# Attention with a SOLU block on one core: an allowance in TensorE's order, VectorE at some casts and low parts, and new wanted times

## The chip, the core and the metric

The kernel runs on one core of a Trainium2 chip. The metric is device time in microseconds from launch to end, the median of several runs. TensorE multiplies matrices into PSUM (eight banks of 128 x 512 fp32). VectorE, ScalarE and GpSimd work on PSUM and SBUF, GpSimd on SBUF alone in this kernel, and SyncE issues the DMAs. Each engine takes its own instructions in the order in which the program has them and waits at semaphores for the others.

## What is computed

```python
factor = 2; scale = 1.0 / np.sqrt(D)                       # B, H, S, D = 4, 8, 1152, 64
q_pool = q.reshape(B, H, S // factor, factor, D).mean(axis=3)
scores = scale * np.matmul(q_pool, k.transpose(0, 1, 3, 2))
attn = np.exp(scores - np.max(scores, axis=-1, keepdims=True))
attn = attn / (np.sum(attn, axis=-1, keepdims=True) + 1e-09)
x = np.matmul(attn, v).transpose(0, 2, 1, 3).reshape(B * S // 2, H * D)   # 2304 x 512

h = x @ w_in                                               # 512 -> 1024
e = np.exp(h - np.max(h, axis=-1, keepdims=True))
solu = h * e / (np.sum(e, axis=-1, keepdims=True) + 1e-09)
mu, var = mean and variance of solu over its 1024 columns
out = ((solu - mu) / np.sqrt(var + 1e-06) * g_ln) @ w_out  # 1024 -> 512
```

q and k are drawn with a large spread, and all inputs and the output are fp32.

## The kernel before

**The work.** There are 32 heads, taken as 16 pairs P. A head has 576 pooled queries and 1152 keys, and its keys are cut into nine blocks of 128. A *step* is one block of keys of one head, so there are 288 steps, s = 9 g + j for block j of head g. To keep fp32's accuracy at TensorE's speed, numbers are split in a high part and a low part (the rest), and products are made of high by high, high by low and low by high.

**One step** (`scores`, from line 958) is this: TensorE makes the scores of 128 keys by 576 queries as two halves of 288 columns, each of two products (`product`; the second product adds the low parts and the shift by the row's maximum). ScalarE takes exponentials: one writes `eh`, the fp16 high part, another writes `e32` (printed as `e`), the same in fp32. GpSimd subtracts (`rest`, line 1006): `e32 - eh`, the *low part*, stored beside `eh`. In some steps `eh` is not a second exponential but a cast of `e32` by VectorE (`cast`, line 996; `use_dve` says in which steps). Then TensorE multiplies `eh`, its low part and the two parts of v (`vhi`, `vlo`) for two or three steps at a time (`values`). In the first steps both halves of a step's scores lie in a pair of banks and one exponential takes all 576 columns (`expo2`, line 989, steps below TP); later one takes 288 columns (`expo`, line 983). `eh` has six buffers, `e32` two. From head 8 on (AH) a low part is written as 512 and 64 columns.

**Before a head's steps** come its maxima (`maxima`): 12 or 15 products of 384 columns into three banks, each reduced by VectorE (line 860), then the transpose of the row maxima (line 869), the shift `c` by VectorE (line 872) and two small DMAs. **Before a pair's steps** come its loads and splits (`pair`): k is transposed and split, q is loaded, pooled by GpSimd (line 606, "q's sum"), transposed and split, and v is scaled by its own largest value and split. For v, the letter VM of the pair says which engines do it: B scales on ScalarE (line 794), C on VectorE (line 796), both with the high part on ScalarE (line 803) and the low part on GpSimd (line 812); with A, ScalarE scales and makes the high part in one (line 801) and VectorE the low part (line 808).

**The token block** (`tokens`) takes 128 rows of x at a time, 18 blocks. A block is 24 products of 512 columns with the parts of w_in, exponentials, statistics, a scaling by g (line 1212), transposes, and 24 products with the parts of w_out. Thirteen blocks are done beside the steps, five after them (the tail). **The weights** (`weight_part`) come in 16 parts; each takes two ScalarE instructions `up` and `un` (line 486), a join on GpSimd (line 493), two VectorE instructions (lines 497, 501), a copy on ScalarE (line 504, `wih` or `woh`) and a subtraction on VectorE.

**What sets the order.** Nothing is written in the order in which it runs. Each piece of work is given to `add` with its engine, an estimated length and a wanted time `at`, counted in steps; `Plan.run` then plays the program forward with these lengths and with `HOP`, an allowance in ns for a signal from one engine to another. Whenever an engine is free, it takes the piece with the smallest `at` whose inputs are there by that play and whose buffers are free; pieces more than `win` steps ahead of the current scores must wait. The instructions are written out in the order that results. So the numbers in `KP` and the lengths change the order of the instructions of every engine, and on the chip only this order is left of them. The wanted times in `KP` are: W (first part of the weights, spacing of the first eight, of the others), M and MA (first block, spacing, length of a block's first products), P (how many steps ahead of a pair's first step k, q and v are prepared and loaded: KA, QA, VA, LK, LQ, LV), N, N1 (maxima: how far ahead, over how many steps), AV (delay of `values`), OF (offsets within a head's end and a block), V0 (v of pair 0), and TP and TX (steps below which scores use paired or extra banks).

## Time and profile before

| | |
|---|---|
| median of 3 runs | 707.68 us (705.69 to 709.21) |
| profiled execution | 707.37 us, its span from first to last instruction 705.1 us |
| busy share of the span | TensorE 95%, weight loads 83%, ScalarE 78%, VectorE 72%, GpSimd 72% |
| chain that ended last | TensorE 66%, VectorE 12%, ScalarE 10%, GpSimd 6%, issue 5% |
| DMA | 75.8 MB, mean 107 GB/s |

The span is the time that the trace covers; the 2.3 us between it and the execution's time lie around it. TensorE's busy time is the union of its matmuls' spans, and these overlap: the next matmul starts while the last is still running out. So a gap in its work is seen as idle time only when it is longer than that overlap. Weight loads are listed apart; a weight load that waits shows that TensorE had to wait for an input, at times without an idle gap among the matmuls. For the other engines too a span is longer than the distance to the next start when the engine is full, and the distance is then what an instruction costs.

### The profile page before, as it was taken

To read this page: it belongs to the slowest core of one execution; us is meant where nothing else is said; L and a number is where in the kernel's file an instruction comes from. 1 tells how busy PE (TensorE), PEld (TensorE's weight loads), DVE (VectorE), ACT (ScalarE), POOL (GpSimd) and SP (SyncE) were. 2 spreads that over 40 slices of the span, in tenths; PEclk is the share of its full clock that TensorE was granted. 3 is DMA by queue.
4 is the path that set the end of the run, shared out by engine and by line. 5 is a ranking of instruction groups with operands and counts; after the bars stand their busy time and mean duration, and the time that the engine had idled before them with its cause. 6 is when DMAs were issued, how large, how long until landed. Compare 5 with 4: busy or idle time off the path is not lost.

```text
span 705.1 us, 19052 instructions
## 1 busy us (share of the span) xinstructions
PE 672.5 (95%) x7151; PEld 582.0 (83%) x7151; DVE 509.0 (72%) x1216; ACT 551.3 (78%) x1366; POOL 507.8 (72%) x651
## 2 busy tenths in 40 slices
PE   9889889989999999999999999999999999999996
PEld 8677778778978888888888988898888898888775
DVE  7798888888878586777868686868686867235452
ACT  3989899988898797878888788888787877763432
POOL 2688899997788787787869686977868677751211
PEclk9999999999999999999999999999999999999999
DMA  5598576965271634546252635444344410010011
GB/s 181 162 211 200 154 190 164 252 143 140 68 163 44 148 90 104 134 93 152 52 138 61 145 85 125 113 91 116 72 121 101 104 34 19 16 24 16 15 31 30
DMA packets 76024, 75.80 MB, mean 107 GB/s; under 512 B 58789, under 2 KB 58909, under 8 KB 75933
## 3 DMA queue, kind: packets, MB, share of 16 engines
q1 hardware_dynamic: 75932, 74.60, 43.7%
q8 instruction: 56, 0.92, 0.6%
q14 instruction: 36, 0.29, 0.1%
HBM read 37.22 MB, written 4.72 MB: 59 GB/s over the span
## 4 chain that ended last, share of the span: by engine, by line
PE 66%; DVE 12%; ACT 10%; POOL 6%; issue 5%; ACTq 0%; DVEq 0%; POOLq 0%
PE bank L419 59%; POOL eh L1006 5%; DVE mx L860 4%; PE bank L1225 2%; ACT e L983 2%; DVE q L422 2%; PE bank L1375 2%; PE bank L628 1%; ACT eh L983 1%; ACT e L989 1%; ACT eh L989 1%; ACT q L722 1%; ACT e L1168 1%; PE bank L712 1%; DVE bank L497 1%
## 5 line engine op out<-in xcount | busy, mean ns | idle before, releaser
L1006 POOL TENSOR_TENSOR eh<-e,eh 128x64 f16<-128x64 f32 (+1 forms) x504 | 405.0, 828 | 109.7 <-ACT e L983 28.8
L860 DVE TENSOR_REDUCE mx<-bank 128x1 f32<-128x384 f32 x420 | 220.5, 548 | 50.5 <-PE bank L419 47.8
L419 PE MATMUL bank<-q,w 128*128 128x288 f32 (+1 forms) x1152 | 238.3, 312 | 6.7 <-ACT e L989 3.3
L419 PEld LDWEIGHTS bank<-q,w 128*128 128x128 f32 (+1 forms) x1152 | 184.6, 191 | 34.8 <-ACT e L983 12.1
L983 ACT ACTIVATE eh<-bank 128x288 f16<-128x288 f32 x392 | 167.0, 429 | 49.1 <-PE bank L419 46.1
L983 ACT ACTIVATE e<-bank 128x288 f32<-128x288 f32 x434 | 183.4, 433 | 16.7 <-POOL eh L1006 13.1
L419 PEld LDWEIGHTS <-eh 128*128 128x128 f16 x4104 | 134.0, 98 | 18.4 <-issue 8.3
L419 PE MATMUL bank<-vhi,eh 128*128 128x65 f16 x2664 | 144.2, 195 | 3.0 <-POOL eh L1006 2.9
L419 PE MATMUL bank<-w,q 128*128 128x384 f32 x390 | 132.9, 367 | 9.8 <-DVE mx L860 5.7
L419 PE MATMUL bank<-vlo,eh 128*128 128x64 f16 x1440 | 140.4, 193 | 0.0
L419 PEld LDWEIGHTS bank<-w,q 128*128 128x128 f32 x390 | 71.7, 190 | 25.6 <-DVE mx L860 13.4
L1208 POOL TENSOR_TENSOR st<-st 128x1 f32<-128x1 f32 x54 | 25.4, 471 | 58.4 <-ACT junk L1195 56.2
L989 ACT ACTIVATE eh<-bank 128x576 f16<-128x576 f32 x70 | 47.5, 680 | 3.5 <-PE bank L419 3.4
L989 ACT ACTIVATE e<-bank 128x576 f32<-128x576 f32 x71 | 48.4, 681 | 0.7 <-POOL eh L1006 0.4
L1156 DVE TENSOR_REDUCE st<-bank 128x1 f32<-128x512 f32 x36 | 24.7, 687 | 25.4 <-PE bank L419 22.5
L422 DVE TENSOR_TENSOR klo<-bank,khi 128x384 fp32r<-128x384 f32 x45 | 24.8, 552 | 19.1 <-ACT khi L631 18.9
L422 DVE TENSOR_TENSOR q<-bank,q 64x384 fp32r<-64x384 f32 (+2 forms) x63 | 28.8, 458 | 12.6 <-ACT q L722 9.7
L419 PE MATMUL bank<-woh,lh 128*128 128x512 f32 x104 | 33.3, 408 | 0.7 <-DVE e L1175 0.7
L419 PE MATMUL bank<-wih,xh 128*128 128x512 f32 x104 | 33.3, 407 | 0.0
L419 PE MATMUL bank<-wil,xh 128*128 128x512 f32 x104 | 32.9, 398 | 0.0
L419 PE MATMUL bank<-wih,xl 128*128 128x512 f32 x104 | 32.3, 397 | 0.0
L419 PE MATMUL bank<-woh,ll 128*128 128x512 f32 x104 | 32.1, 397 | 0.0
(128 smaller groups left out, 1025.1 us busy)
## 6 DMA issues: line engine op xcount, KB each, us to landing
qt<-in_q_dram SPq DMA_DIRECT2D x16, 576.0 KB
kt<-in_k_dram SPq DMA_DIRECT2D x32, 288.0 KB
vt<-in_v_dram SPq DMA_DIRECT2D x16, 576.0 KB
w<-w SPq DMA_DIRECT2D x32, 288.0 KB
w<-khi SPq DMA_DIRECT2D x30, 288.0 KB
w<-klo SPq DMA_DIRECT2D x30, 288.0 KB
out_dram<-o SPq DMA_DIRECT2D x36, 128.0 KB
raw<-in_moe_w_in_dram SPq DMA_DIRECT2D x8, 511.6 KB
```

Of the source, the lines that this page charges most:

```text
L419: nc.tensor.matmul(out=o, lhsT=a, rhs=b, start=first, stop=last, skip_group_check=True)
L422: nc.vector.tensor_tensor(out=o, in0=a, in1=b, op=ALU.subtract)
L497: nc.vector.tensor_scalar(out=ps.bitcast(I32), in0=tl["raw", n][:, :, 0], scalar1=5, scalar2=128 << 23, op0=ALU.logical_shift_right, op1=A ...
L628: nc.tensor.transpose(ps[:, c, :], tl["kt", P][:, 3 * i + c].rearrange("p h d -> p (h d)"), ident)
L860: nc.vector.tensor_reduce(out=tl["mx", g][:, m, c:c + 1], in_=tl["nps", (g, m, c)], op=ALU.max, axis=AXX)
L983: nc.scalar.activation(out=tl[name, (g, j)][:, f * HALF:(f + 1) * HALF], in_=tl[tn(j, f), (g, j, f)], func=ACTF.Exp, scale=ESC,)
L989: nc.scalar.activation(out=new((name, (g, j)), [128, SQ * 4 // mybir.dt.size(dtype)], dtype)[:, 0:SQ].rearrange("p (f i) -> p f i", f=2), ...
L1006: nc.gpsimd.tensor_tensor(out=e[:, o:o + c.stop - c.start], in0=e32[:, c], in1=e[:, c], op=ALU.subtract)
L1156: nc.vector.tensor_reduce(out=st(f), in_=tl[H_[f]], op=ALU.max, axis=AXX)
L1208: nc.gpsimd.tensor_tensor(out=st(o), in0=st(a), in1=nhalf if b is None else st(b), op=op)
L1225: nc.tensor.transpose(ps[:, c, :], tl[E][:, o:o + 128], ident)
L1375: plan.warm = lambda i: nc.tensor.transpose(bank[:, i, 0:128], ident, ident)
```

## The change

The numbers of `KP` are set anew, four names are new in it, and three pieces of code use them:

- **HP** = [145872, 60]: on work that TensorE takes up after 145.872 us of the play, 60 ns are added to the allowance for a signal from another engine to TensorE. It has no instruction of its own.
- **CD** is now a list of ranges. Casts by VectorE: steps 25 and 50 in 6 to 72, and every twentieth step from 80 to 280 (13). Before it was every tenth from 70 to 280 (22).
- **SD** names steps whose low part VectorE makes: 25, 38, 50 and 63. Its estimated length is VectorE's for 576 columns and 250 ns more.
- **MA** is the spacing of the first blocks; it has the same value as M's.
- VM: v is scaled on VectorE for the pairs 0, 1, 2, 3, 8, 12, 13 (before 1, 2, 3, 12), on ScalarE as B for 6, 7, 9, 10, 11, 14 (before 0, 6, 7, 8, 10, 11, 13), as A for 4, 5, 15 (before 4, 5, 9, 14, 15).

```diff
-KP = {'W': [2, 4.47, 5], 'step': 0.66, 'M': [78.27, 15.99, 7.61], 'TX': 112, 'TP': 71, 'win': 4.11, 'P': [22.92, 18.81, 13.57, 24.85, 27.38, 30.44], 'N': [10.43, 7], 'AV': 3.97, 'CD': [67, 10], 'VM': 'BCCCAABBBABBCBAA', 'AH': 8, 'OF': [5.14, 2.61, 11.19, 1.04, 2.66], 'N1': 12.32, 'warm': 1, 'ws': 1.3, 'GR': 1, 'GG': 10, 'b_eh': 6, 'b_w1': 4, 'V0': -55.58, 'VF': 1, 'QD': [0, 1], 'L0': 0.97, 'F': 0, 'DL': 2000}
+KP = {'W': [2, 5.8, 5], 'step': 0.73, 'M': [78.27, 15.99, 7.64], 'TX': 106, 'TP': 72, 'win': 4.6, 'P': [22.99, 20.5, 12.83, 24.85, 25.26, 30.44], 'N': [10.46, 6.38], 'AV': 4.07, 'CD': [[6, 73, 4], [73, 288, 5]], 'SD': [[15, 73, 8], [73, 288, 0]], 'VM': 'CCCCAABBCBBBCCBA', 'AH': 8, 'OF': [5.31, 2.61, 11.94, 0.25, 1.01], 'N1': 11.36, 'warm': 1, 'ws': 1.3, 'GR': 1, 'GG': 10, 'b_eh': 6, 'b_w1': 4, 'V0': -50.92, 'VF': 1, 'QD': [0, 1], 'L0': 0.97, 'F': 0, 'HP': [145872, 60], 'DL': 2000, 'MA': 15.99}
...
+        PAD = KP.get("HP", [0, 0])
+        pad = PAD[1]
...
-                            t = max(t, x.end + hop[x.engine][e] + load)
+                            t = max(t, x.end + hop[x.engine][e] + load + (pad if e == "PE" and t > PAD[0] else 0))
...
                     if o.engine == e and not m.deps[o]:
                         hop = 0
+                    elif e == "PE" != o.engine and t > PAD[0]:
+                        hop += pad
...
-    def use_dve(s):
-        a, b = KP.get("CD", [100, 0])
-        return s >= a and b > 0 and (s * b) % 100 < b
+    def use_dve(s, key):
+        return any(a <= s < z and (s * b) % 100 < b for a, z, b in KP[key])
...
-                add("POOL", POOL(SQ) + 149 * joined, a, lambda j=j: rest(j), [("eh", (g, j)), ("e32", (g, j))], [("eh", (g, j), "l")])
+                low = ([("eh", (g, j)), ("e32", (g, j))], [("eh", (g, j), "l")])
+                if use_dve(NJ * g + j, "SD"):
+                    add("DVE", DVE(SQ) + 250 + 65 * joined, a + 0.3, lambda j=j: rest(j, nc.vector), *low)
+                else:
+                    add("POOL", POOL(SQ) + 149 * joined, a, lambda j=j: rest(j, nc.gpsimd), *low)
```

The new code shifts line numbers: line 989 of before is 992 in the changed kernel, 1006 is 1009, 996 is 999, 419 is 423.

**ScalarE at the first steps.** Names: `up` and `un` are of a part of the weights, `eh` and `e` are exponentials of steps 0 to 2, `vt` is v of pair 0 being scaled, `vhi` its high part. Before:

```order
L486 ACTIVATE up<-raw,ebias 128x512
L989 ACTIVATE eh<-bank 128x576
L989 ACTIVATE e_314<-bank 128x576
L794 ACTIVATE vt<-vt,vs 128x1152
L989 ACTIVATE eh<-bank 128x576
L803 CAST vhi_75<-vt 128x18x64
```

and with the change:

```order
L490 ACTIVATE up<-raw,ebias 128x512
L992 ACTIVATE eh<-bank 128x576
L992 ACTIVATE e_314<-bank 128x576
L992 ACTIVATE eh<-bank 128x576
L992 ACTIVATE e_328<-bank 128x576
L490 ACTIVATE un<-raw,ebias 128x512
L807 CAST vhi_75<-vt 128x18x64
```

The scaling of v has left ScalarE's row, and two more exponentials stand ahead of v's high part.

**VectorE at step 25** (the third pair's v is scaled there, too). Before:

```order
L796 TENSOR_SCALAR vt<-vt,vs 128x1152
L872 TENSOR_SCALAR c_1171<-bank 4x128
L860 TENSOR_REDUCE mx<-bank 128x1 x6
L497 TENSOR_SCALAR bank<-raw 128x512
L501 TENSOR_TENSOR bank<-bank,up 128x512
```

and with the change:

```order
L876 TENSOR_SCALAR c_1113<-bank 4x128
L800 TENSOR_SCALAR vt<-vt,vs 128x1152
L864 TENSOR_REDUCE mx<-bank 128x1 x2
L999 CAST eh<-e_1176 128x576
L864 TENSOR_REDUCE mx<-bank 128x1
L1009 TENSOR_TENSOR eh<-e_1176,eh 128x576
L864 TENSOR_REDUCE mx<-bank 128x1
L501 TENSOR_SCALAR bank<-raw 128x512
```

The cast and the low part of step 25 now stand among the maxima on VectorE, and the shift `c` stands ahead of the scaling.

**TensorE at step 203**, where a head's maxima are transposed (`m`), the next head's maxima begin (`w,q`, 384 columns) and scores follow (`q,w`, 288 columns). Before:

```order
L419 MATMUL bank<-q_7012,w_6941 128x288
L419 MATMUL bank<-q_7013,w_0_73 128x288
L869 MATMUL bank<-ident,m_7984 4x128
L419 MATMUL bank<-w_7642,q_7744 128x384 x3
L419 MATMUL bank<-q_7012,w_6941 128x288
```

and with the change:

```order
L873 MATMUL bank<-ident,m_7983 4x128
L423 MATMUL bank<-q_6976,w_6944 128x288
L423 MATMUL bank<-q_6977,w_0_73 128x288
L778 MATMUL bank<-ident,am 128x128
L423 MATMUL bank<-w_7660,q_7749 128x384
L423 MATMUL bank<-q_6976,w_6944 128x288
```

Three products of the next maxima stood right behind the transpose; now scores stand there and one such product behind them.

## Rows read from the trace of the kernel before

**Rows 1.** Busy time by stretch (stretch, its length, then us and count).

```profile
core 0: us, PE busy (x) PEld busy (x) DVE busy (x) ACT busy (x) POOL busy (x), PEclk, DMA share, GB/s
...
20.00:159.00 139.00, 122.09 (x1539) 102.04 (x1538) 118.45 (x250) 130.85 (x239) 124.73 (x94) 0.99 0.75 188
159.00:200.00 41.00, 39.92 (x451) 34.60 (x450) 34.45 (x80) 34.48 (x102) 33.41 (x48) 0.96 0.50 120
200.00:624.00 424.00, 417.33 (x4640) 367.04 (x4640) 305.57 (x778) 350.19 (x957) 330.59 (x462) 1.00 0.40 93
624.00:705.00 81.00, 74.75 (x393) 60.51 (x392) 35.67 (x80) 29.62 (x61) 15.31 (x33) 0.99 0.11 25
```

**Rows 2.** Waits, 20 to 159 us: us in total, times, longest.

```profile
POOL eh L1006 <- ACT e L989: 11.8, 10, 5.2
PEld bank L419 <- DVE mx L860: 10.8, 23, 1.7
...
PEld bank L419 <- ACT e L989: 7.8, 17, 1.9
```

**Rows 3.** Waits, 159 to 624 us.

```profile
ACT eh L983 <- PE bank L419: 46.0, 71, 1.7
...
PEld bank L419 <- ACT e L983: 12.1, 37, 0.8
...
PEld bank L419 <- DVE mx L860: 3.4, 10, 0.6
```

**Rows 4.** Line 989: shortest, median, longest ns, first and last start.

```profile
L989 ACT ACTIVATE e<-bank x71: 631/672/792, 21.6 to 154.1; 128x576 f32<-128x576 f32 x71
```

**Rows 5.** ScalarE in order of time, three places (start, length).

```profile
22.12 1.25 ACT L794 ACTIVATE vt<-vt,vs 128x1152 f32<-128x1152 f32 x1
23.27 0.63 ACT L989 ACTIVATE eh<-bank 128x576 f16<-128x576 f32 x1
...
105.27 0.65 ACT L989 ACTIVATE e<-bank 128x576 f32<-128x576 f32 x1
105.80 0.77 ACT L486 ACTIVATE up<-raw,ebias 128x512 int32<-128x512 int8 x1
106.46 0.76 ACT L486 ACTIVATE un<-raw,ebias 128x512 int32<-128x512 uint8 x1
...
110.34 0.59 ACT L504 CAST woh<-bank 128x512 fp32r<-128x512 f32 x1
110.82 0.76 ACT L486 ACTIVATE up<-raw,ebias 128x512 int32<-128x512 int8 x1
```

**Rows 6.** Lines 996, 1212 (columns as rows 4) and 1006's group (busy, mean).

```profile
L996 DVE CAST eh<-e x22: 441/627/2086, 154.8 to 612.8; 128x576 f16<-128x576 f32 x22
...
  POOL eh L1006: 8.8, 11
...
L1212 DVE SCALAR_TENSOR_TENSOR e<-e,st,g_sb x13: 1269/1397/2199, 193.7 to 621.4; 128x1024 f32<-128x1024 f32 x13
L1212 DVE SCALAR_TENSOR_TENSOR et<-et,st,g_sb x5: 1309/1311/1311, 644.3 to 691.8; 128x1024 f32<-128x1024 f32 x5
...
L1006 POOL TENSOR_TENSOR eh<-e,eh 128x576 f16<-128x576 f32 x72 | 93.6, 1320 | 16.4 <-ACT e L989 11.8 <-PE bank L419 2.6 <-DVE q L422 1.4
```

**Rows 7.** VectorE and TensorE in order of time at step 203.

```profile
444.20 1.57 DVE L796 TENSOR_SCALAR vt<-vt,vs 128x1152 f32<-128x1152 f32 x1
...
444.46 0.27 PE L869 MATMUL bank<-ident,m 128*4 128x128 f32 x1
444.49 0.59 PE L419 MATMUL bank<-w,q 128*128 128x384 f32 x2
...
445.70 0.27 DVE L872 TENSOR_SCALAR c<-bank 4x128 fp32r<-4x128 f32 x1
...
446.02 0.44 PE L419 MATMUL bank<-w,q 128*128 128x384 f32 x1 [0.94 <-DVE c L872]
```

**Rows 8.** SyncE and GpSimd in order of time: the second q load.

```profile
9.70 0.33 SPq L561 DMA_DIRECT2D qt<-in_q_dram  x1
...
15.68 1.41 POOL L606 TENSOR_TENSOR qt<-qt 128x576 f32<-128x576 f32 x1 [10.29 <-DMA qt<-in_q_dram]
```

More of the change, by code (lines that the diff above doesn't have):

```diff
@@ L1001, in scores, with rest @@
         LO = 2 * SQ - MQ if joined else SQ
-        def rest(j):
+        def rest(j, eng):
             e, e32 = tl["eh", (g, j)], tl["e32", (g, j)]
             for o, c in ((SQ, slice(MQ, SQ)), (LO, slice(0, MQ))) if joined else ((SQ, slice(0, SQ)),):
-                nc.gpsimd.tensor_tensor(
+                eng.tensor_tensor(
                     out=e[:, o:o + c.stop - c.start], in0=e32[:, c], in1=e[:, c], op=ALU.subtract
@@ L1068, in scores @@
             a = at + j
-            by_dve = use_dve(NJ * g + j)
+            by_dve = use_dve(NJ * g + j, "CD")
             exact = whole(NJ * g + j)
@@ L1369, in attention_solu_moe @@
             jobs.append((t, lambda n=n, t=t, s=src, k=key, d=dsts, tail=tail: token_job(n, t, s, k, d, MR, tail)))
-            t += MP
+            t += MP if n > 4 else KP.get("MA", MP)
         jobs.append((t + 100, lambda: prev[0](t)))
```

## The prediction

> **What bounds the kernel now.** I read the busy time by stretch first [rows 1]. Three stretches differ. From 20 to 159 us the kernel does attention alone, with the split of the weights beside it: ScalarE is busy 130.85 of 139.00 us (94%), GpSimd 124.73, VectorE 118.45, and TensorE's 122.09 is its lowest share of any stretch. From 159 to 624 us TensorE is busy 39.92 + 417.33 of 465 us, because the token products now fill it, and ScalarE has 34.48 + 350.19 of 465 (83%). After 624 us only the last five blocks of tokens are left.
>
> So there are two limits. In the first stretch it is ScalarE: GpSimd's longest wait there is for ScalarE's exponentials (11.8 us), and TensorE's weight loads wait 7.8 us for the same instructions and 10.8 us for VectorE's maxima [rows 2]. In the second stretch the direction is reversed: ScalarE waits 46.0 us for scores [rows 3], so nothing taken from ScalarE there is worth anything by itself. What is lost there are TensorE's short waits, shown at its weight loads: 12.1 us in 37 waits for ScalarE and 3.4 us in 10 for VectorE [rows 3]. The busy share hides most of them, since a matmul's span runs on after the next could have started.
>
> **Early ScalarE work (the main term).** The steps with paired banks, steps 0 to 70, have their exponentials of e from 21.6 to 154.1 us [rows 4], 1.89 us a step. I counted ScalarE's instructions up to that of step 70 in both orders. The changed one has one multiplication of v less (pair 0 now has letter C, VectorE), one eh less (two casts for steps 25 and 50 are VectorE's, before it was that of step 70), and two parts of the weights less, since W spaces them by 5.8 steps and not 4.47: 13 pairs of up/un and four of the `woh` copies instead of 15 and six. What each takes of ScalarE's queue is the distance to the next start [rows 5]: the multiplication 22.12 to 23.27, 1.15 us; a paired exponential 105.27 to 105.80, 0.53; up 0.66, and un, the same size, the same; the copy 110.34 to 110.82, 0.48. That is 1.15 + 0.53 + 2 x (0.66 + 0.66 + 0.48) = 5.3 us. GpSimd loses as much: four low parts of 1.32 us [rows 6] (steps 25, 38, 50, 63) and two joins of the same parts. VectorE gets these four, two casts and the multiplication, and loses its three instructions on each of the two parts.
>
> How much of 5.3 us reaches the clock? All, if ScalarE is never behind anything else. Its idle 8.15 us of 139 and the maxima in [rows 2] say that it sometimes is. I take 0.8, near its 94% share: **-4.2 us**, from -5.3 to -1.0 (the waits stay and swallow the rest).
>
> **The two parts that are put off.** They fall in steps 73 to 91 and add 3.6 us to ScalarE there; nine more eh fall to ScalarE in all (22 casts before, 13 now; after step 72 it was 21 and is eleven). In 159 to 200 us ScalarE is idle for 6.5 of 41 us [rows 1], which hides it; if not, it is 3.6 us. No token product needs `woh` before step 104 in either order. I take **+0.5**, from 0 to +3.6.
>
> **VectorE's part in it.** The casts that are left out were short only in name. The same cast took from 441 to 2086 ns, and GpSimd waited 8.8 us for eleven of them [rows 6]. [Rows 7] shows what such an operation does to TensorE, with v's multiplication in its place: VectorE ran it for 1.57 us from 444.20, the shift c stood behind it until 445.70, its bank stayed taken, and TensorE, with two of the maxima's products out, started the third at 446.02, after 0.94 us of idleness. Ten casts fewer after step 72 are a gain. Against that stand three more multiplications of that kind (pairs 0, 8, 13) and two fewer of VectorE's low parts of v. The order at step 203 also changed: the transpose of m now has other products behind it. I take **-0.5**, from -2 to +1.
>
> The low part itself is not in this trace. The nearest VectorE operation with both inputs in SBUF is the scaling by g, 1397 ns beside a working GpSimd, 2199 at most, and 1311 without it, on 1024 columns [rows 6]. For 576 columns that is 0.74 us without a wait, and with the longest wait (0.89) 1.63; four are 3 to 6.5 us. VectorE is idle 20.5 of 139 us there, so I cost them at nothing on the path; without that cover they are the second rival.
>
> **The allowance of 60 ns.** It acts on the order alone, from 145.9 us on: TensorE takes a product up only when its input would be there 60 ns earlier, else the next one. The 47 waits of [rows 3] are 0.33 us in the mean. If each becomes 60 ns shorter that is 2.8 us; if other work fills all of them it is the whole 15.5; if the new order only moves them, it is nothing. I take half of the 47 x 60 ns, **-1.5 us**, from -5 to +1.5. A product put off costs TensorE nothing so long as there is other work: after the scores of step 286 the old order has 276 token matmuls left and the new one 272. The wider window, TX, TP, N and OF change which filler comes next and not how much there is: by step 72 the maxima counted are 129 in both, by step 144 the token matmuls are 168 in both. So the sum of TensorE's work is the same, and the tail too, where the order differs by a few transposes: 0, from -1 to +1.
>
> **The clock.** In 159 to 200 us the granted share is 0.96, in 20 to 159 us 0.99 [rows 1]; that is 1.6 and 1.4 us of lost full clock, short stretches at 1.2 GHz after a time of waiting. They may go or come back elsewhere: nothing in the sum, 1.5 us in the range.
>
> **Sum.** -4.2 + 0.5 - 0.5 - 1.5 = -5.7 us against the profiled execution, 707.37 us with a span of 705.1, so 701.7. The median of the runs is 0.3 above that execution: **702.0 us**.
>
> **Rivals.** *The relief is swallowed.* ScalarE's work goes down but its waits grow by as much, because VectorE (85% busy in the stretch, with more put upon it) sets the pace through the maxima and the low halves of k. For it speaks that the 10.8 us of weight loads waiting for maxima are the larger sum in [rows 2]; against it that GpSimd's 11.8 us point to ScalarE. Then 0.2 of 5.3 us is left and the later terms cancel: 706.6, within 0.5%. Chance 0.22. That the allowance does nothing, the case that the change does not do what it says, leaves 703.5 and is inside the forecast.
>
> *The four low parts block two engines.* Here each would wait for a whole low part on GpSimd (1.32 us) and hold GpSimd for its own 0.74: 4 x 2.06 = 8.2 us. With half of it on the path the time is 706. [Rows 6] shows waits of that order at single instructions (2086, 2199 ns), but a median of 0.09 us over the undisturbed 1311. Chance 0.05. The Trainium skill, page "SBUF — State Buffer", section "Who interferes with whom", speaks for this rival and against the change: it says that a VectorE instruction with two SBUF inputs contends with a GpSimd instruction that reads SBUF, and that whoever issues first has the shared pair for the whole instruction while the other fully blocks. By that rule the longest rows of [rows 6] are full blocks, and no run here shows yet how often one happens; the median agrees with it only if most pairs miss each other.
>
> *The q loads come too close: the slower side.* The change issues the load of q later (LQ 25.26, was 27.38) but wants the pooled q earlier (QA 20.5, was 18.81). Counted in steps, the third load is issued at 10 and its sum stands on GpSimd at 12; before it was 4 and 16. Three further pairs are as close: 62/64, 80/82, 97/98 (before 62/65, 79/82, 96/99). GpSimd takes its queue in order, so low parts stand behind the sum, the two buffers of e32 stay taken, and ScalarE stops. The only load whose landing the trace shows took from 9.70 to 15.68 us, 6.0 us, and GpSimd stood idle for 10.29 [rows 8]; two steps are 3.8 us. At 6.0 us each of the four would hold GpSimd for 2.2; if the first, amid the weights' transfers (the DMA engines are 0.75 busy in the stretch [rows 1]), takes twice as long, 8.2. With three quarters of 14.8 us on the path the time is 702 + 11 = 713. It decides from about 9 us in all. Against it: three of the four stood three steps apart before and GpSimd's list of waits in [rows 2] and [rows 3] has no DMA in it. Chance 0.10.
>
> **How the numbers follow.** Forecast 0.60 at 702.0; swallowed 0.22 and blocked 0.05, both within 0.5%; late loads 0.10, slower; 0.03 for a gain beyond the forecast's own bounds. 0.5% is 3.5 us, about what a measurement of this kernel can tell from no change. Faster 0.63, same 0.27, slower 0.10. The low ends together (-5.3, 0, -2, -5 and 1.5 of clock) would give 694; they will not all meet, so 696.5. The high end takes in both middle rivals and stops short of the last: 709.0.
>
> **What would show it.** The last paired exponential, now that of step 71, should start near 154.1 + 1.9 - 4.2 = 151.8 us; after 154 the main term is wrong. GpSimd should nowhere wait for a q load after the second; one wait of over 2 us is the third rival. The four low parts on VectorE should be near 0.8 us; over 1.4 is the second. In the long stretch weight loads should wait fewer than 47 times or under 15.5 us for ScalarE and VectorE, or the allowance did nothing. The prediction fails if the time from step 72 to the end is longer than before by more than 2 us, since I forecast it shorter by 1.5.

## The result, and the profile after

The changed kernel took **713.82 us** (median of 6 runs, 711.87 to 715.18), the kernel before beside it 707.80: a ratio of 1.0085 (95% interval 1.0056 to 1.0113). Run again later (e5 below) it took 709.41 us (12 runs, 706.38 to 715.20) against 707.77: 1.0027 (1.0005 to 1.0049). So it is 1.6 to 6 us slower, where 5.7 us were to be gained. Its profiled execution took 715.18 us with a span of 713.1; it lies at the slow end of its spread, and so the stretches below show the loss larger than the medians do.

A step starts with the first of its four score products of 288 columns; counting these in the trace gives the time of each stretch of steps (us):

| | before | after | change | forecast |
|---|---|---|---|---|
| start of step 0 | 19.9 | 20.1 | +0.2 | 0 |
| steps 0 to 72 | 139.2 | 146.1 | **+6.9** | -4.2 |
| steps 72 to 108 | 73.3 | 77.5 | **+4.2** | +0.5 |
| steps 108 to 287 | 392.1 | 389.8 | -2.3 | -2.0 |
| step 287 to the end of the span | 80.6 | 79.6 | -1.0 | 0 |

The late steps came out near the forecast, though not for the reason forecast (see below); the early ones and those of the first token block did not. Busy time by stretch, cut at the same steps as [rows 1] (columns as there):

```profile
20.00:166.00 146.00, 127.74 (x1542) 109.52 (x1541) 124.42 (x250) 127.47 (x229) 118.02 (x88) 0.93 0.67 168
166.00:208.00 42.00, 37.99 (x414) 32.28 (x414) 34.68 (x79) 37.37 (x102) 35.58 (x48) 0.96 0.63 150
208.00:633.00 425.00, 419.97 (x4666) 372.76 (x4666) 299.64 (x774) 357.85 (x983) 335.91 (x467) 1.00 0.40 93
```

ScalarE and GpSimd have indeed less to do in the early stretch (127.47 of 146.00 us, [rows 1] had 130.85 of 139.00), and yet it is 7 us longer: no engine is as full as ScalarE was. VectorE has 250 instructions there as before, and is busy 6 us longer with them. TensorE's granted clock fell from 0.99 to 0.93. The place where most of the time is lost is step 50. Here are the rows of after in order of time, engine by engine (start, length):

```profile
119.48 1.46 POOL L610 TENSOR_TENSOR qt<-qt 128x576 f32<-128x576 f32 x1
120.86 1.31 POOL L1009 TENSOR_TENSOR eh<-e,eh 128x576 f16<-128x576 f32 x1
122.10 1.29 POOL L497 TENSOR_TENSOR up<-up,un 128x512 f32<-128x512 f32 x1
123.32 1.30 POOL L1009 TENSOR_TENSOR eh<-e,eh 128x576 f16<-128x576 f32 x1
127.14 1.28 POOL L1009 TENSOR_TENSOR eh<-e,eh 128x576 f16<-128x576 f32 x1 [2.52 <-PE bank L423]
...
120.28 4.67 DVE L999 CAST eh<-e 128x576 f16<-128x576 f32 x1 [0.72 <-ACT e L992]
124.87 0.55 DVE L426 TENSOR_TENSOR klo<-bank,khi 128x384 fp32r<-128x384 f32 x1
125.33 0.27 DVE L876 TENSOR_SCALAR c<-bank 5x128 fp32r<-5x128 f32 x1
125.53 0.74 DVE L1009 TENSOR_TENSOR eh<-e,eh 128x576 f16<-128x576 f32 x1
...
126.36 0.65 ACT L992 ACTIVATE e<-bank 128x576 f32<-128x576 f32 x1 [2.96 <-DVE eh L1009]
...
125.47 0.64 PE L423 MATMUL bank<-w,q 128*128 128x384 f32 x2 [3.52 <-DVE klo L426]
```

The cast of step 50 (L999) takes 4.67 us, where a cast of this size takes 0.44 us at its best [rows 6]. Nearly all that time GpSimd works: q's sum, a low part, a join, another low part, each starting as the one ahead of it ends. The cast is done 0.3 us after the last of them, when GpSimd has run dry. I call that being *shut out*. Behind the cast stand the low half of k, the shift c and the low part of the same step; TensorE stands still for 3.52 us waiting for the first, ScalarE for 2.96 us, because the low part has not given e's buffer back. Then TensorE's clock goes to half (columns as in the windows above):

```profile
126.40:129.80 3.40, 3.40 (x44) 3.32 (x41) 2.66 (x6) 1.86 (x4) 1.28 (x1) 0.50 0.50 99
129.80:136.70 6.90, 5.76 (x73) 4.70 (x70) 6.06 (x13) 6.63 (x14) 5.01 (x4) 0.99 1.01 245
136.70:143.50 6.80, 6.80 (x55) 5.83 (x56) 4.60 (x13) 5.84 (x10) 5.04 (x4) 0.50 0.74 204
```

The granted 0.50 is the 1.2 GHz level, and it comes twice after the stop. Steps 48 to 60, in which all this lies, took 27.8 us, before 21.4.

Not every such operation is shut out for so long. The low part of step 25 came up beside a join, too; it ended 0.6 us after that one instruction, and GpSimd's row went on, with its next instruction 0.5 us longer than elsewhere (2.81 us; 2.31 for the low part of v of other pairs):

```profile
74.29 1.51 POOL L497 TENSOR_TENSOR up<-up,un 128x512 f32<-128x512 f32 x1
75.75 2.81 POOL L816 TENSOR_TENSOR vlo<-vt,vhi 128x1152 f16<-128x1152 f32 x1
...
75.03 1.37 DVE L1009 TENSOR_TENSOR eh<-e,eh 128x576 f16<-128x576 f32 x1
```

The Trainium skill, page "SBUF — State Buffer", section "Who interferes with whom", says that VectorE's casts can, and its operations on two SBUF inputs do, contend with GpSimd for a shared pair of ports, and that whoever issues first has the pair for the whole instruction while the other fully blocks. The trace agrees that VectorE blocks; at step 25 it blocks for one instruction of GpSimd, as the page has it, and at step 50 through four.

### The profile page after: what moved, and what is told of

The parts are those of the page before. It is cut to its first block, busy times and chain, and to the rows that moved or that the text cites. A ratio compares the mean times of both kernels' runs of the same rounds, so it can differ in the third digit from the quotient of the medians.

```text
span 713.1 us, 19073 instructions
## 1 busy us (share of the span) xinstructions
PE 677.7 (95%) x7151; PEld 592.5 (83%) x7151; DVE 508.7 (71%) x1212; ACT 557.6 (78%) x1382; POOL 508.4 (71%) x649
## 4 chain that ended last, share of the span: by engine, by line
PE 46%; DVE 5%; ACT 3%; issue 2%; POOL 1%; ACTq 0%; POOLq 0%
PE bank L423 42%; PE bank L1232 2%; DVE mx L864 1%; POOL eh L1009 1%; ACT e L986 1%; PE bank L632 1%; PE bank L1143 1%; ACT eh L986 1%; DVE e L1182 1%; DVE et L1219 1%; ACT junk L1202 1%; POOL st L1215 0%; DVE q L426 0%; DVE et L1182 0%; PE bank L716 0%
## 5 line engine op out<-in xcount | busy, mean ns | idle before, releaser
L1009 POOL TENSOR_TENSOR eh<-e,eh 128x64 f16<-128x64 f32 (+1 forms) x500 | 399.3, 823 | 118.3 <-POOL eh L1009 27.4
L423 PE MATMUL bank<-q,w 128*128 128x288 f32 (+1 forms) x1152 | 246.0, 315 | 7.1 <-ACT e L986 4.3
L423 PEld LDWEIGHTS bank<-q,w 128*128 128x128 f32 (+1 forms) x1152 | 190.9, 193 | 33.4 <-ACT e L986 10.8
L986 ACT ACTIVATE eh<-bank 128x288 f16<-128x288 f32 x410 | 175.3, 433 | 50.4 <-PE bank L423 47.1
L986 ACT ACTIVATE e<-bank 128x288 f32<-128x288 f32 x432 | 184.4, 437 | 13.0 <-POOL eh L1009 9.9
L423 PEld LDWEIGHTS <-eh 128*128 128x128 f16 x4104 | 136.0, 99 | 13.2 <-issue 5.4
L423 PE MATMUL bank<-vhi,eh 128*128 128x65 f16 x2664 | 146.3, 196 | 0.3 <-DVE eh L1009 0.3
L423 PE MATMUL bank<-w,q 128*128 128x384 f32 x390 | 135.4, 372 | 9.7 <-DVE klo L426 3.9
L423 PE MATMUL bank<-vlo,eh 128*128 128x64 f16 x1440 | 142.4, 195 | 0.4 <-POOL vlo L816 0.4
L423 PEld LDWEIGHTS bank<-w,q 128*128 128x128 f32 x390 | 73.5, 194 | 26.2 <-DVE mx L864 11.0
L423 PE MATMUL bank<-wol,lh 128*128 128x512 f32 x104 | 32.1, 397 | 0.0
```

The lines of the kernel that those rows point to most:

```text
L423: nc.tensor.matmul(out=o, lhsT=a, rhs=b, start=first, stop=last, skip_group_check=True)
L986: nc.scalar.activation(out=tl[name, (g, j)][:, f * HALF:(f + 1) * HALF], in_=tl[tn(j, f), (g, j, f)], func=ACTF.Exp, scale=ESC,)
L1009: eng.tensor_tensor(out=e[:, o:o + c.stop - c.start], in0=e32[:, c], in1=e[:, c], op=ALU.subtract)
```

## The experiments

Theories: (1) VectorE's early casts and low parts are **shut out** by GpSimd; (2) the **wanted times** set anew are worse, whatever VectorE does; (3) the **clock**: the half-clock stretches are themselves the loss. All kernels were timed beside the kernel before. Steps 0 to 72, 72 to 108, 108 to 287 and the profiled time are of the profiled execution; medians in us. Of the times expected, those of e1, e3, e4 and e10 were missed to the better side (e1, e3 and e4 were counted from 713.8, and e5 gave 709.41 for the same kernel), those of e7 and e9 by 0.3 us or less, and those of e8, e13 and e15 to the worse side.

| run | 0–72 | 72–108 | 108–287 | profiled | median | ratio to before (95%) |
|---|---|---|---|---|---|---|
| before | 139.2 | 73.3 | 392.1 | 707.37 | 707.5 to 708.2 | |
| after | 146.1 | 77.5 | 389.8 | 715.18 | 713.82 | 1.0085 (1.0056–1.0113) |
| e5 after again | 146.1 | 77.5 | 389.9 | 715.20 | 709.41 | 1.0027 (1.0005–1.0049) |
| e1 early casts as reductions | 140.6 | 76.3 | 389.7 | 708.14 | 707.13 | 0.9990 (0.9972–1.0007) |
| e9 and low parts as reductions | 134.7 | 77.1 | 389.9 | 703.05 | 706.15 | 0.9975 (0.9957–0.9993) |
| e6 before + early casts, low parts | 142.2 | 73.1 | 392.3 | 710.89 | 711.05 | 1.0050 (1.0038–1.0062) |
| e4 after without these | 137.2 | 80.2 | 389.6 | 708.72 | 706.63 | 0.9988 (0.9971–1.0005) |
| e7 the same, W 4.47 | 140.2 | 72.3 | 390.3 | 704.12 | 704.25 | 0.9961 (0.9947–0.9974) |
| e11 the same, v of pair 0 as before | 140.4 | 72.6 | 390.2 | 704.19 | 704.98 | 0.9968 (0.9955–0.9980) |
| e8 after, v of pair 0 as before | 151.0 | 75.9 | 389.9 | 718.08 | 718.02 | 1.0146 (1.0128–1.0164) |
| e3 after without HP | 142.7 | 76.3 | 389.8 | 710.44 | 707.65 | 1.0008 (0.9985–1.0030) |
| e2 before + HP | 140.5 | 72.9 | 391.5 | 708.29 | 706.96 | 0.9996 (0.9979–1.0014) |
| e12 after, idle transposes | 147.7 | 74.5 | 391.0 | 714.75 | 714.54 | 1.0098 (1.0072–1.0123) |
| e10 before, half the late casts | 136.9 | 73.3 | 391.5 | 704.15 | 702.28 | 0.9935 (0.9914–0.9956) |
| e13 before without step 70's cast | 136.0 | 73.0 | 392.3 | 703.93 | 705.92 | 0.9975 (0.9961–0.9989) |
| e14 before, casts as reductions | 137.6 | 71.7 | 392.2 | 704.22 | 705.11 | 0.9959 (0.9943–0.9975) |
| e15 e10, casts as reductions | 136.9 | 73.5 | 391.3 | 703.80 | 704.01 | 0.9952 (0.9937–0.9967) |
| e16 e7, casts as reductions | 139.9 | 72.3 | 390.6 | 703.93 | 704.03 | 0.9950 (0.9935–0.9966) |

**Is the shutting out the cause? e1, e9 and e6.** In e1 the two early casts get another form in the same place of the order:

```diff
-            nc.vector.tensor_copy(out=eh, in_=e32)
+            nc.vector.tensor_reduce(out=eh, in_=e32.rearrange("p (n u) -> p n u", u=1), op=ALU.max, axis=AXX)
```

> The changed kernel with its order of instructions untouched; only the two casts of steps 25 and 50 are made by VectorE as a maximum over a single element (a reduction of 576 x 1) instead of a copy, same input and output. Theory 1 (shut out): the cast of step 50, 4.67 us in the profile of the changed kernel, waits for GpSimd's unbroken row of instructions; a reduction does not. Then both instructions take 0.6 to 0.8 us, the scores of step 60 start by 138.5 us (143.7 in the changed kernel, 135.3 before), and the time is 708 to 710 us (713.8 less 4 to 6). Theory 2 (the new wanted times made the early order worse, the cast is only the place where it shows): step 60 at 142 us or later, time 712 us or more. Theory 3 (the clock): the half clock at 126 to 143 us stays though the wait is gone, and the time is 711 to 713.

The casts took 0.74 and 0.75 us, TensorE's stop fell from 3.52 to 2.37 us, and the median is 707.13. The shutting out moved one instruction on: the low part of step 50, which takes 0.74 us in after, now took 3.62. In e1 (VectorE, GpSimd, TensorE):

```profile
117.81 0.75 DVE L1001 TENSOR_REDUCE eh<-e 128x576 f16<-128x576 f32 x1 [0.72 <-ACT e L992]
119.14 3.62 DVE L1015 TENSOR_TENSOR eh<-e,eh 128x576 f16<-128x576 f32 x1
...
118.39 1.29 POOL L1015 TENSOR_TENSOR eh<-e,eh 128x576 f16<-128x576 f32 x1
119.64 1.28 POOL L497 TENSOR_TENSOR up<-up,un 128x512 f32<-128x512 f32 x1
120.87 1.27 POOL L1015 TENSOR_TENSOR eh<-e,eh 128x576 f16<-128x576 f32 x1
...
123.75 0.55 PE L716 MATMUL bank<-ident,qt 128*128 128x128 f32 x3 [2.37 <-DVE klo L426]
```

It too ends only after GpSimd's row of work has ended (at 122.14 us; the low part at 122.76). So e9 takes this away as well; the four early low parts are written by a reduction of e, the subtraction left out:

```diff
-                eng.tensor_tensor(out=eh_low, in0=e32, in1=eh, op=ALU.subtract)
+                eng.tensor_reduce(out=eh_low, in_=e32.rearrange("p (n u) -> p n u", u=1), op=ALU.max, axis=AXX)   # VectorE's four
```

> The changed kernel in the same order of every engine; VectorE's two early casts and its four early low parts are made as reductions over one element. The subtraction is left out of these four low parts (they are written as e itself), with the same bytes read from e and the same bytes written. Theory 1 (a cast or a subtraction of VectorE on SBUF is shut out while GpSimd works): nothing is shut out now, all six take 0.5 to 0.9 us, steps 48 to 60 take 21 to 23 us (27.8 in the changed kernel, 24.3 with the casts alone replaced, where the low part of step 50 took 3.62 us), and the time is 703 to 706. Theory 2 (the place of these six in VectorE's queue is what costs, whatever they take): 707 to 710, steps 48 to 60 stay above 24 us.

```profile
115.82 0.75 DVE L1001 TENSOR_REDUCE eh<-e 128x576 f16<-128x576 f32 x1 [0.73 <-ACT e L992]
117.15 0.73 DVE L1016 TENSOR_REDUCE eh<-e 128x576 f16<-128x576 f32 x1
...
115.02 1.41 POOL L610 TENSOR_TENSOR qt<-qt 128x576 f32<-128x576 f32 x1
116.40 1.28 POOL L1021 TENSOR_TENSOR eh<-e,eh 128x576 f16<-128x576 f32 x1
117.65 1.27 POOL L497 TENSOR_TENSOR up<-up,un 128x512 f32<-128x512 f32 x1
```

The order is that of after on every engine, the same bytes are written beside the same GpSimd work (the reduction reads e alone, where the subtraction reads eh too), and none of the six waits. Steps 48 to 60 took 20.7 us (after 27.8), steps 0 to 72 took 134.7, and the median is 706.15. Theory 1 holds, and theory 2 falls for this stretch, since the order is the same. The Trainium skill (page "SBUF — State Buffer", section "Who interferes with whom") says that tensor_reduce never contends on this chip; the 0.75 us here and the shortest, median and longest of 22 in e14 (721, 752, 754 ns) agree. e6 is the counter-test, this part alone put into the kernel before:

```diff
 kernel before, with use_dve of after
-'CD': [67, 10]
+'CD': [[6, 73, 4], [73, 288, 10]], 'SD': [[15, 73, 8]]
```

> The kernel before with one part of the change alone: VectorE's casts at steps 25 and 50 and its low parts at steps 25, 38, 50 and 63; all else as before. Theory 1 (these operations are shut out by GpSimd, and the low parts beside them): step 72 starts later than before, by 1 to 6 us, the operation that is shut out is seen as a cast or low part of over 1.4 us, and the time is 709 to 714. Theory 2 (the wanted times set anew place them badly, the operations themselves do no harm): in the order of before they cost nothing, 706 to 708, or gain up to 2 us since ScalarE and GpSimd have less to do.

It took 3.3 us more (711.05 against 707.77), in the middle of what theory 1 gave. But not all else is as before: its list of casts has no step 70 either, and taking that cast away gives 2.3 us by itself (e13 below), so the six cost about 5.5 us here. The shut-outs are there, at step 50 both the cast and the low part, each behind one instruction of GpSimd:

```profile
123.12 1.65 DVE L999 CAST eh<-e 128x576 f16<-128x576 f32 x1
...
125.16 1.67 DVE L1009 TENSOR_TENSOR eh<-e,eh 128x576 f16<-128x576 f32 x1
```

Over all six they come to 3.2 us beyond the shortest such cast (0.44 us) and low part (0.74); what adds the rest, the place in VectorE's queue or the clock (5.1 us of full clock lost in steps 0 to 72, in e13 none), no run separates.

**The wanted times: e4, e7, e11, e8.** e4 is after with `'CD': [[73, 288, 5]], 'SD': []`.

> The changed kernel without the four low parts on VectorE and without its casts of steps 25 and 50 (GpSimd and ScalarE make them again); order as the play gives it, equal up to about step 24. Theory 1: step 60 starts by 139 us, time 708 to 710. Theory 2: no better than 712. By the prediction's own sum (each low part relieves GpSimd by 1.32 us, each cast ScalarE by 0.53) it would be slower than the changed kernel by 0 to 1.5 us.

Without VectorE's early six, steps 0 to 72 took 137.2 us: 9 us better than after's slow profiled execution (by the medians e4 is 2.8 to 7.2 us better), as theory 1 says. But steps 72 to 108 rose to 80.2. These hold the two parts of the weights that W = 5.8 puts off; e7 is e4 with `'W': [2, 4.47, 5]`.

> The changed kernel without VectorE's early casts and low parts (706.63 us in the earlier run), and with the spacing of the first weight parts at 4.47 again, so that they are no longer put off into the first token block. If the put-off parts cost the 4 to 5 us that steps 72 to 90 lost (38.7 us in the earlier run, 34.2 before), that stretch is back at 34 to 35 us, and the time is 702 to 704, less up to 2.6 us that the two parts cost again before step 72. If they cost nothing there, it stays at 706 to 709 and the stretch at 38 us.

72 to 108 fell by 7.9 to 72.3 us, below before's 73.3, 0 to 72 rose by 3.0, and the median is 704.25, 2.4 us less. Every kernel with W = 5.8 took 74.5 to 80.2 us there, every one with 4.47 took 71.7 to 73.5. So the put-off parts cost more where they land than they save earlier. The rows of after there show ScalarE with a copy of the weights, `up`, a token block's exponentials (L1175) and squares (L1202) in one row of work almost without a gap, and TensorE waiting for the exponentials (L986) that stand behind the squares and behind a second copy and free its banks:

```profile
198.39 0.59 ACT L508 CAST woh<-bank 128x512 fp32r<-128x512 f32 x1 [0.56 <-DVE bank L505]
198.87 0.77 ACT L490 ACTIVATE up<-raw,ebias 128x512 int32<-128x512 int8 x1
199.53 0.68 ACT L1175 ACTIVATE e<-bank,st 128x512 f32<-128x512 f32 x1
...
202.02 1.19 ACT L1202 ACTIVATE junk<-e,st 128x1024 f16<-128x1024 f32 x1
...
204.05 0.59 ACT L508 CAST woh<-bank 128x512 fp32r<-128x512 f32 x1
...
203.95 0.54 PE L423 MATMUL bank<-q,w 128*128 128x288 f32 x2 [1.20 <-ACT e L986]
205.30 0.85 PE L423 MATMUL bank<-q,w 128*128 128x288 f32 x2 [0.81 <-ACT e L986]
```

e8 is after, and e11 is e7, each with v of pair 0 on ScalarE again (`'VM': 'BCCCAABBCBBBCCBA'`).

> The changed kernel with v of pair 0 scaled on ScalarE again (letter B), all other numbers as changed; pieces after it move a little. In the profile after, step 6 started 1.9 us later than before, with VectorE's scaling of v taking 1.86 us beside a low part on GpSimd and v's high part behind it. If the scaling costs that, step 6 is back at about 31.6 us and the time is 1 to 2 us below that of the changed kernel in this call. If the late step 6 is a half-clock stretch at 31 us and not the scaling, nothing is gained, or up to 1 us is lost to ScalarE's longer queue.

> The changed kernel without VectorE's early casts and low parts, with the weights spaced by 4.47 (704.25 us in the earlier run), and with v of pair 0 on ScalarE. Steps 0 to 6 took 13.5 us with it on VectorE beside GpSimd, 11.8 us before and in the earlier run with it on ScalarE. If that is the scaling's price and nothing behind it takes it back: steps 0 to 6 at 11.8 us, time 702 to 703.5. If ScalarE's work sets the pace of the steps behind (my main term), the 1.15 us put back on it cancel it: 704 to 705.5.

Steps 0 to 6 came back to 11.8 us in both (13.4 in after, where the scaling took 1.86 us beside a low part). Not all of the 1.6 us is the scaling's price: in e3 and e16 it took 1.86 and 1.90 us as well, but no half-clock stretch fell there, and steps 0 to 6 took 12.3. In e11 the next ones gave it back (12 to 24 took 25.6 us, in e7 22.8): 704.98 against 704.25. e8 I had wrong by 10 us, and it shows theory 1 again: the order shifted a little, and two of the six were shut out, a low part behind one instruction of GpSimd and the cast behind four (GpSimd, VectorE, TensorE):

```profile
72.29 2.51 POOL L816 TENSOR_TENSOR vlo<-vt,vhi 128x1152 f16<-128x1152 f32 x1
...
73.04 2.37 DVE L1009 TENSOR_TENSOR eh<-e,eh 128x576 f16<-128x576 f32 x1
...
75.93 1.37 PE L423 MATMUL bank<-w,q 128*128 128x384 f32 x3 [2.33 <-DVE mx L864]
...
123.59 4.69 DVE L999 CAST eh<-e 128x576 f16<-128x576 f32 x1
...
129.60 0.69 PE L423 MATMUL bank<-w,q 128*128 128x384 f32 x1 [3.47 <-DVE mx L864]
```

What a shut-out costs thus hangs on what happens to stand beside it, and a change that looks like one of ScalarE's load can move it. Why steps 60 to 72 took 26.6 us in e8 (22.5 in after) stays open.

**The allowance: e2 and e3.** e2 is before with `'HP': [145872, 60]`, e3 after without HP.

> The kernel before with the allowance of 60 ns from 145.9 us on and nothing else of the change; its order is that of before up to about step 73. Theory (the allowance saves what the prediction put on it): weight loads wait less than 47 times or 15.5 us between 159 and 624 us, and the time is 705.5 to 707 (-1 to -2.3). Rival (the gain of 2.3 us seen in the long stretch of the changed kernel comes from the fewer casts or from chance in the order): 707.5 or more.

> The changed kernel without the allowance; its order is that of the changed kernel up to about step 73. If the allowance saves 1 to 2.3 us: 715 to 716. If it does nothing: 713.8 within 0.7. In both cases the cast of step 50 again takes over 3 us and step 60 starts at 142 to 145 us.

Alone, the allowance does nothing that can be measured: e2's 706.96 lies in the range given to it, but the kernel before beside it took 707.47 (0.9996, 0.9979 to 1.0014). e3 has the same early order as after, with the cast of step 50 again at 4.64 us, and yet its first 72 steps were 3.4 us shorter. Its granted clock was higher:

```profile
20.00:163.00 143.00, 124.88 (x1543) 106.12 (x1543) 123.70 (x251) 127.65 (x230) 118.49 (x88) 0.96 0.68 173
```

That is 0.96 against 0.93 in after: in the same order the clock falls more often in one execution than in another, and with it go the 3.4 us.

**The clock: e5 and e12.** e5 is the changed kernel once more; e12 has `'warm': 288`, idle transposes wherever the play sees TensorE idle.

> The changed kernel once more, beside the others of this call, since the same early order without the 60 ns gave 707.65 us and the changed kernel 713.82 in another session. If the loss belongs to the order, this run gives 713 to 715 again and the cast of step 50 is again over 4 us. If it belonged to the session (half-clock stretches that come and go, 27.3 us of them in the first profile and 6.8 us in that of before), it gives 707 to 710, with fewer such stretches.

> The changed kernel with idle transposes of a constant written into TensorE's order wherever the play sees it idle, at all steps (before and after only at the last ones); they move the order of other pieces a little. Theory 3 (the loss is the clock's: TensorE waits, falls to half clock, and the half-clock stretches, 27.3 us in the profile after, are the loss): fewer such stretches, clock over 0.99, time 703 to 707. Theory 1 (the waits themselves are the loss): the play does not know of the shut-outs, the cast of step 50 or a low part still takes over 3 us if it meets GpSimd, and the time is 708 to 714 or worse, as the transposes delay what becomes ready.

e5's profiled execution repeats after's (715.20 us, cast of step 50 at 4.65), as expected if the loss belongs to the order, while its median of 709.41 lies in the range given to the session: its twelve runs go from 706.38 at a mean granted clock of 0.990 to 715.20 at 0.981. In the three traces of this early order (after, e5, e3) the stop at step 50 is the same and the clock is not; so it is likely, though not shown for the executions without a trace, that the order sets up the stops and the clock decides how much a run pays for them. In e12 the clock was 0.995 over the execution and the time was 714.54 all the same:

```profile
20.00:168.00 148.00, 136.99 (x1779) 125.45 (x1778) 124.91 (x258) 128.93 (x234) 121.31 (x90) 0.98 0.69 172
```

The cast took 4.52 us, and one half-clock stretch of 6.8 us still followed it. With the clock higher (0.98 against 0.93) nothing was gained; but TensorE carried some 240 matmuls more in this stretch, so the price of the clock alone stays open. Theory 3 as the whole cause falls: e9 lost the stops and regained the clock (0.99 in its steps 0 to 72) without any filler.

**The late casts: e10, e13, e14, e15, e16.** e10 is before with `'CD': [[73, 288, 5]]`.

> The kernel before with one part of the change alone: after step 72 VectorE casts at every twentieth step, not at every tenth (13 casts, before 22, and none at step 70). The changed kernel's steps 108 to 287 took 389.8 us, before 392.1. If the casts are what this came from (my term of fewer casts, -0.5 us, was too small), the stretch is 389 to 390.5 us here and the time 705 to 706.5. If it came from the wanted times, the stretch stays at 391.5 to 393 and the time at 707 to 708.

(e10 has 11 casts; the 13 above are the changed kernel's, two early ones among them.) At 702.28 us it is the fastest of all kernels here, and of the 3.2 us that its profiled execution gained 0.6 lie in steps 108 to 287 (391.5) and 2.3 before step 72, around step 70. There the kernel before has a shut-out of its own (GpSimd, VectorE, TensorE, before):

```profile
154.03 1.30 POOL L493 TENSOR_TENSOR up<-up,un 128x512 f32<-128x512 f32 x1
155.28 1.28 POOL L1006 TENSOR_TENSOR eh<-e,eh 128x576 f16<-128x576 f32 x1
156.96 1.27 POOL L1006 TENSOR_TENSOR eh<-e,eh 128x576 f16<-128x576 f32 x1 [0.40 <-DVE eh L996]
...
154.79 2.09 DVE L996 CAST eh<-e 128x576 f16<-128x576 f32 x1
...
158.80 0.44 PE L419 MATMUL bank<-w,q 128*128 128x384 f32 x1 [1.61 <-DVE mx L860]
```

The longest cast of [rows 6], 2086 ns, is this one, and its end comes when GpSimd has nothing left but the low part that waits for this very cast. e13 takes away this cast alone (`'CD': [[73, 288, 10]]`); e14, e15 and e16 keep the order of before, e10 and e7 and make every cast a reduction, as in e1.

> The kernel before, where only the cast of step 70 goes back to ScalarE; the other 21 casts on VectorE stay as they are. In the trace of before that cast took 2.09 us from 154.79 and TensorE stood still for about 1.8 us behind it. If this one instruction is what the run with half of the casts gained (702.28 us), the time is 702 to 704 here and steps 60 to 72 take 21.5 to 22.5 us (23.7 before). If the nine later casts were the gain, the time stays at 705.5 to 707.5.

> The kernel before in the same order of every engine, its 22 casts on VectorE made as reductions over one element; nothing is left out. In the changed kernel the same replacement made every cast 0.74 us. If it is GpSimd shutting the casts out, none is over 0.8 us now (before 0.44 to 2.09), TensorE's stop behind step 70 goes, and the time is 703.5 to 706. If the place of the cast in the queue is what costs, and the mean of 0.78 us before is what counts, 707 to 708.

> The kernel before with VectorE casting at every twentieth step after step 72 (702.28 us in the earlier run), and these casts made as reductions. Their mean there was 0.69 us, so reductions of 0.74 us gain nothing in the mean; only if single casts are still shut out is there a gain: 700.5 to 703, else 702 to 703.5.

> The changed kernel without VectorE's early casts and low parts and with the weights spaced by 4.47 (704.25 us in the earlier run), its late casts made as reductions in the same order. The casts took 0.72 us in the mean there, so nothing is to be had in the mean: 703.5 to 705. If shut-outs of single casts cost it something, 702 to 703.5.

One instruction, moved to ScalarE, gave 2.3 us (705.92 against 708.22). Steps 60 to 72 fell to 21.9 us as expected, but the median did not reach 702 to 704, so that cast is not all that e10 gained. Changing only the form of the 22 casts gave 3.1 (705.11). The order was the same in e14 and the mean cast hardly shorter (746 ns, before 777): it is the long ones that cost, not the mean. e15 and e16 gained nothing over e10 and e7 that can be told from no change, as expected where no early cast is left. Whether e10's further 3 us over e13 are due to the other ten casts (21 in e13, 11 in e10) stays open: the interval of e15, with as few casts, overlaps both.

## Why the prediction was wrong, point by point

From the 702.0 us forecast to the 709.4 and 713.8 measured lie 7.4 to 11.8 us. As an estimate from the medians, the shut-outs are 3.3 to 7.7 of it (e9 against after), the put-off parts 2.4 (e4 against e7), and the allowance's 1.5 did not come.

**The bound.** In [rows 1] ScalarE is the fullest engine of the early stretch. What I missed is that VectorE's short work on SBUF can hold up TensorE and ScalarE at any step.

**Early ScalarE work (-4.2).** The relief is there once nothing is shut out, but not all of it. e9, in the order of after, took 4.5 us less than before for steps 0 to 72, yet only 1.3 us less than e13, which is before without its cast of step 70, and 2.2 less than e10 and e15, which are without it, too. By the sign I named, the last paired exponential, e9 stands at 154.27 us, 1.7 us better than [rows 4] with a step added, and not 4.2. So the relief is some 1.3 to 2.2 us, near the "waits swallow the rest" end of my bounds, and the other 2 to 3 come with the cast at step 70, which I counted only as an eh of 0.53 us more for ScalarE. The two put-off parts by themselves did give what I put on them there: 3.0 us (e4 against e7), 0.8 x 3.6 forecast. In the changed kernel the sign failed outright:

```profile
L992 ACT ACTIVATE e<-bank x72: 635/657/726, 21.8 to 166.0; 128x576 f32<-128x576 f32 x72
```

166.0, where "after 154" was to mean that the term is wrong.

**The step that failed most** is the price of VectorE's six early operations. I costed the casts at nothing and the low parts at nothing "on the path", with VectorE's 20.5 us of idleness as cover, and put the second rival at 0.05 because the scaling by g in [rows 6] waits 0.09 us at the median. That row is from steps after 193 us, where GpSimd's work has gaps; in the first stretch it is busy 90% of the time in unbroken rows. And I let a shut-out last for one GpSimd instruction (1.32 us). Most did, but the cast of step 50 waited through four (4.67 us), its low part in e1 through three (3.62) and the cast of step 70 in before through two (2.09). What decides whether VectorE comes in after one instruction or not stays open. The four low parts did take 0.74 to 1.37 us in after, under the 1.4 that I had named as the sign of this rival; one cast was enough. The rival's mechanism was right, but it applied to casts as well as low parts. Measured, the term that I put at nothing is 3.3 (e9 against e5's median of after) to 7.7 us (against the first median). The rival's own 4 us (706 against 702) lie within that by luck, as it counted four low parts of 2.06 us, where one cast did most.

I had the evidence: the 2086 ns of [rows 6] come with a first start at 154.8 us, which is that same cast. I took the group's longest row as a bound and did not look at what stood beside it.

**The two put-off parts (+0.5, bounds 0 to 3.6)** added 3.8 (e9 against before) to 6.9 us (e4 against before) in steps 72 to 108, where other wanted times differ, too; with W alone changed it is 7.9 (e4 against e7), half-clock stretches included. The 6.5 us of ScalarE's idleness in the stretch were taken as cover, but in the rows shown the parts land beside the token block's exponentials, where ScalarE has almost none. Even the upper bound was too low, as it priced ScalarE's time and not TensorE's stops and clock behind it (5.1 us of full clock lost there in e4, none in e7).

**Fewer casts (-0.5).** That steps 108 to 287 came out at -2.3, where terms three and four together forecast -2.0, is luck. Fewer casts alone gave -0.6 there (e10), and the allowance -0.6 (e2) or, taken out of the changed kernel, nothing (e3 has the same 389.8). The rest goes with the wanted times and VM, for which I had put nothing; no run takes them apart. For the whole kernel, the casts were worth 2.3 us (that of step 70) to 5.3 (eleven) in the order of before; that of step 70 was in no wait that I priced.

**The allowance (-1.5)** gave nothing that can be measured (e2 leaves at most 1.5 us of gain). The sign that I named was met (weight loads waited 36 times for 15.2 us, [rows 3] had 47 times and 15.5), but it was no sign of the allowance: e3, without it, has 36 times and 15.6 us.

```profile
PEld bank L423 <- ACT e L986: 10.8, 24, 1.4
...
PEld bank L423 <- DVE mx L864: 4.4, 12, 0.8
```

**The clock (0, 1.5 in the range).** In 20 to 166 us after lost 0.07 x 146 = 10.2 us of full clock, against 1.4. In after two half-clock stretches follow the stop at step 50, and e9, without that stop, has none in steps 48 to 60; so it belongs to the term that brings the stop, and not beside the sum.

**The other rivals.** The q loads did not hurt: no row of GpSimd's waits names one after the second. The relief was partly swallowed, as said. The slow side came true, but not by the late loads to which its 0.10 belonged: two mechanisms that I had, one as a rival at 0.05 and one as a term of +0.5, met in the same kernel. From step 72 to the end the time was 0.9 us longer than before (546.9 us, before 546.0), within the 2 us that I had named as the limit, but not 1.5 shorter.

## What to carry to other kernels

Before work is moved to VectorE on the ground that it is idle, look at what GpSimd does at that moment: a cast or a subtraction from SBUF to SBUF can wait through one GpSimd instruction or, in an unbroken row, through up to four (4.67 us here), and everything behind it in VectorE's queue waits too. Read the longest member of such a group with its neighbours, not the mean; where the operation must stay, a form that was never kept waiting here (a reduction over one element, 0.72 to 0.75 us at all 22 places) mends it without touching the order. Work that is put off is to be priced at the place where it lands, by who waits there, and not by the idle share of the stretch.

## What the runs showed of the hardware that I had not expected

- A VectorE cast or subtraction was kept waiting through several consecutive GpSimd instructions (four in after, 4.67 us; three in e1, 3.62 us) and not only through the one that ran when it came up. Among the casts and low parts in the traces of all kernels this happened at steps 50 and 70 alone; elsewhere, as at step 25 of after, VectorE waited for one at most. GpSimd lost less: an instruction of its that ran beside a low part of VectorE took about 0.5 us longer (a join in e8 1.80 us, 1.28 elsewhere; the low part of v in after 2.81, 2.31 elsewhere).
- The same program in the same order showed a granted clock of 0.979 to 0.990 over an execution, and 706.4 to 715.2 us with it. The kernel before lay between 703.0 and 710.8 in all sessions.
- One stop of 3.5 us was followed by two stretches of 1.2 GHz, of 3.4 and 6.8 us, with 6.9 us of full clock between them.
